# First-block loads gathered on the sync queue, and the stores of h moved, in a GELU layer with its gradients

## The chip, the cores and the metric

The kernel runs on one core of a Trainium2 chip. The metric is the device time of one execution in microseconds; lower is better. The engines are TensorE (PE in the profile, its weight loads PEld), VectorE (DVE), ScalarE (ACT), GpSimd (POOL) and SyncE (SP). DMAs are issued from SP, ACT or POOL; each of the three has a queue of its own, and all are carried out by the core's 16 DMA engines.

## The reference

A dense layer with GELU between two matrices, forward and backward, in bfloat16:

```python
B, S, D, F = 1, 2048, 448, 1792

def _fwd_reference(x, w1, b1, w2, b2):
    h = jnp.einsum("bsd,df->bsf", x, w1) + b1
    h = _gelu(h)                                   # tanh form
    return jnp.einsum("bsf,fd->bsd", h, w2) + b2

def reference(x, w1, b1, w2, b2, grad_out):
    _out, _vjp = jax.vjp(_f, x, w1, b1, w2, b2)    # _f is _fwd_reference
    return (_out, *_vjp(grad_out))                 # out, gx, gw1, gb1, gw2, gb2
```

## The kernel before

The 2048 rows are cut into four blocks of 512 (NB), and F into seven pairs of 128-row tiles (NPAIR), so there are 28 steps (NSTEP), step g being pair c of block b. The instructions of each engine stand in the order in which the code writes them (the schedule is manual), so every engine and every queue works through its own list in that order and waits where an operand is missing.

In step g, `M1(g + 1)` makes u = x w1 of the next step on TensorE (L200, 8 matmuls), ACT and DVE form h (kept transposed in hT, a ring of 12 pairs) and the pieces of GELU's derivative, `M4(g)` makes q = grad_out w2^T (L209, 8 matmuls), `dve_gate` multiplies q by the derivative into ghT, a ring of 14 pairs, and `run_pieces` (L262) adds 8 to 16 products to the output rows ("o" units: h times w2) and to the rows of x's gradient ("g" units: gh times w1T). In the first block only "o" units run, two products each per step, so that step g reads the w2 tiles 2g and 2g+1. "g" units, which read w1T, begin in step 7, the first of the second block.

M1 reads the transposed x block and w1; M4 reads the transposed grad_out block and w2T, a transposed copy of w2. `load_xg` brings a block of x or grad_out by two transposing DMAs on SP (L131, L132), `load_w2T` the columns f0:f1 of w2T by two on SP (L142, L143), `load_w1T` tiles of w1T by one on SP (L149). `load_w1` brings columns of w1 by two plain DMAs on a queue that it is given (L135, L136), and `load_w2` tiles of w2 by one (L139). In the kernel before, w1's first 256 columns and b1 come by ACT's queue, all other pieces of w1 and w2 by POOL's. POOL also sets the lower rows of w2T's last slice to zero after each piece of w2T has landed (`zero_w2T`, L146) and a row of ones under each block of x (`ones_row`, L152).

`store_h` writes one pair of h to DRAM from POOL (L238, 256 KB), and it stands three steps behind its step: `if g >= LAG: store_h(g - LAG)` with LAG = 3, the last three after the loop. POOL also stores the finished rows of both outputs (L281), two units at a time. `turn_gh` (L243) transposes gh on SP, SBUF to SBUF.

After the loop POOL loads all of x and grad_out (L352, L353), SP transposes h back from DRAM (L365), TensorE finishes the last block's units and makes the two weight gradients (L401, L409 and L420), DVE sums the bias gradients.

Of the kernel before, what the change touches and what calls it, by code (L numbers as in the profile page):

```python
# [18 lines left out]
def kernel(  # L19
# [15 lines left out]
    nc = tc.nc  # L35
    P = 128
    B, S, D = x.shape
    F = w1.shape[1]
    assert B == 1
    NS = S // P  # L40
    NF = F // P
# [7 lines left out]
    NPAIR = NF // 2  # L49
    assert DL == 64 and F % 256 == 0 and S % SB == 0 and NPAIR == 7 and NB == 4  # L50
    NSTEP = NB * NPAIR
# [44 lines left out]
    def xq(b):  # L96
        o = (b % 2) * 2 * KD * SB
        return xg_flat[:, o:o + KD * SB].rearrange("p (k s) -> p k s", k=KD)

    def gq(b):  # L100
        o = ((b % 2) * 2 + 1) * KD * SB
        return xg_flat[:, o:o + KD * SB].rearrange("p (k s) -> p k s", k=KD)
# [5 lines left out]
    def hT(g):  # L108
        return ring(hT_flat, HR, g)
# [19 lines left out]
    def load_xg(src, dst, b):  # L129
        rows = slice(b * SB, (b + 1) * SB)  # L130
        nc.sync.dma_start_transpose(out=dst[:, KF, :], in_=src[rows, DOV:D])  # L131
        nc.sync.dma_start_transpose(out=dst[:, 0:KF, :], in_=src[rows, 0:KF * P])  # L132

    def load_w1(eng, f0, f1):
        eng.dma_start(out=w1_sb[:, 0:KF, f0:f1], in_=w1[0:KF * P, f0:f1].rearrange("(k p) f -> p k f", p=P))  # L135
        eng.dma_start(out=w1_sb[DL:P, KF, f0:f1], in_=w1[KF * P:D, f0:f1])  # L136

    def load_w2(eng, t0, t1):
        eng.dma_start(out=w2_sb[:, t0:t1, :], in_=w2[t0 * P:t1 * P, :].rearrange("(t p) d -> p t d", p=P))  # L139

    def load_w2T(f0, f1):
        nc.sync.dma_start_transpose(out=w2T_sb[:, 0:KF, f0:f1], in_=w2[f0:f1, 0:KF * P])  # L142
        nc.sync.dma_start_transpose(out=w2T_sb[:, KF, f0:f1], in_=w2[f0:f1, DOV:D])  # L143

    def zero_w2T(f0, f1):
        nc.gpsimd.memset(w2T_sb[0:DL, KF, f0:f1], 0.0)  # L146

    def load_w1T(t0, t1):
        nc.sync.dma_start_transpose(out=w1T_sb[:, t0:t1, :], in_=w1[:, t0 * P:t1 * P])  # L149

    def ones_row(b):
        nc.gpsimd.memset(xq(b)[0:1, KF, :], 1.0)  # L152
# [4 lines left out]
    load_xg(x2, xq(0), 0)  # L157
    load_w1(nc.scalar, 0, 256)
    nc.scalar.dma_start(out=w1_sb[0:1, KF, :], in_=b1.rearrange("(o f) -> o f", o=1))
    load_w1(nc.gpsimd, 256, 512)  # L160
    ones_row(0)
    load_w2T(0, 256)
    load_xg(g2, gq(0), 0)
    load_w2(nc.gpsimd, 0, 2)
    load_w1(nc.gpsimd, 512, 768)
    pw = psum_a.tile([P, SB], F32, name="acc")
    for i in range(16):
        nc.tensor.matmul(pw[:], lhsT=warm[:, 0:P], rhs=warm, start=True, stop=True)
    zero_w2T(0, 256)
    load_w2(nc.gpsimd, 2, 6)  # L170
    load_w1(nc.gpsimd, 768, 1280)
    load_w2T(256, 768)
    zero_w2T(256, 768)
    load_w1(nc.gpsimd, 1280, F)
    load_w2(nc.gpsimd, 6, NF)
    load_w2T(768, F)
    zero_w2T(768, F)
    nc.gpsimd.dma_start(out=b2_bc[:], in_=b2.rearrange("(o d) -> o d", o=1).to_broadcast((P, D)))
    load_w1T(0, 4)
    load_xg(x2, xq(1), 1)  # L180
    ones_row(1)
    load_xg(g2, gq(1), 1)
    load_w1T(4, 8)
    load_w1T(8, 12)
# [3 lines left out]
    def blk(g):  # L188
        return divmod(g, NPAIR)
# [4 lines left out]
    def M1(g):  # L194
        b, c = blk(g)
        for h in range(2):
            fc = slice((2 * c + h) * P, (2 * c + h + 1) * P)
            u = psum_u.tile([P, SB], F32, name="u")
            for kt in range(KD):
                nc.tensor.matmul(u[:], lhsT=w1_sb[:, kt, fc], rhs=xq(b)[:, kt, :], start=(kt == 0), stop=(kt == KD - 1))  # L200
            u_of[g, h] = u

    def M4(g):
        b, c = blk(g)
        for h in range(2):
            fc = slice((2 * c + h) * P, (2 * c + h + 1) * P)
            q = psum_g.tile([P, SB], F32, name="q")
            for kt in range(KD):
                nc.tensor.matmul(q[:], lhsT=w2T_sb[:, kt, fc], rhs=gq(b)[:, kt, :], start=(kt == 0), stop=(kt == KD - 1))  # L209
            g_of[g, h] = q  # L210

    def act_first(g):
        for h in range(2):
            nc.scalar.activation(out=hT(g)[:, h, :], in_=u_of[g, h][:], func=ACT.Gelu_apprx_tanh)  # L214
            nc.scalar.activation(out=A_of(g)[:, h, :], in_=u_of[g, h][:], func=ACT.Square, scale=math.sqrt(3.0 * GELU_C * GELU_A))  # L215

    def dve_first(g):
        for h in range(2):
            nc.vector.scalar_tensor_tensor(out=B_of(g)[:, h, :], in0=A_of(g)[:, h, :], scalar=3.0 * GELU_C,  # L219
                                           in1=u_of.pop((g, h))[:], op0=ALU.add, op1=ALU.mult)  # L220
        nc.vector.scalar_tensor_tensor(out=p_of(g), in0=A_of(g), scalar=GELU_C, in1=hT(g), op0=ALU.add, op1=ALU.mult)  # L221

    def act_second(g):
        nc.scalar.activation(out=t_of(g), in_=B_of(g), func=ACT.Tanh, scale=-1.0 / 3.0)  # L224
        nc.scalar.activation(out=p_of(g), in_=p_of(g), func=ACT.Copy, bias=-0.5)  # L225

    def dve_second(g):
        nc.vector.tensor_scalar(out=t_of(g), in0=t_of(g), scalar1=1.0, scalar2=None, op0=ALU.add)
        nc.vector.tensor_tensor(out=t_of(g), in0=t_of(g), in1=p_of(g), op=ALU.mult)  # L229

    def dve_gate(g):
        for h in range(2):
            nc.vector.scalar_tensor_tensor(out=ghT(g)[:, h, :], in0=t_of(g)[:, h, :], scalar=1.0,  # L233
                                           in1=g_of.pop((g, h))[:], op0=ALU.add, op1=ALU.mult)

    def store_h(g):
        b, c = blk(g)
        nc.gpsimd.dma_start(out=hT_dram_v[:, 2 * c:2 * c + 2, b * SB:(b + 1) * SB], in_=hT(g))  # L238

    def turn_gh(b, c0, c1):  # L240
        o = ((b * NPAIR + c0) % GR) * 2 * SB
        n = 2 * (c1 - c0)
        nc.sync.dma_start_transpose(out=gh_nat[:, b, 2 * c0:2 * c1, :].rearrange("p t (j f) -> p (t j) f", f=P),  # L243
                                    in_=ghT_flat[:, o:o + n * SB])
# [40 lines left out]
    def run_pieces(units):  # L285
        for un in units:
            if un.piece():
                full.append(un)

    def flush():  # L290
        while full:
            evict(full.pop(0))
# [13 lines left out]
    for b in range(NB):  # L306
        for i, (c0, c1) in enumerate(GROUPS):
# [1 line left out]
            if b == NB - 1:  # L309
                at = b * NPAIR + (4, 5, 6)[i]  # L310
            turns.setdefault(at, []).append((b, c0, c1))
    LAG = 3

    M1(0)
    act_first(0)
# [3 lines left out]
    for g in range(NSTEP):  # L319
        b, c = blk(g)  # L320
        pieces = [U[k] for k in seq[b] for _ in range(NF)]
        n = len(pieces)
        own = pieces[n * c // NPAIR:n * (c + 1) // NPAIR]
        grown = [U[k] for k in grow[b] for _ in range(2)]
        cut = len(own) // 2
        if g + 1 < NSTEP:
            M1(g + 1)
            act_first(g + 1)
            dve_first(g + 1)
        if g >= LAG:  # L330
            store_h(g - LAG)
        flush()
        run_pieces(own[:cut] + grown[:len(grown) // 2])
        M4(g)
        dve_gate(g)
        flush()
        run_pieces(own[cut:] + grown[len(grown) // 2:])
        if g + 1 < NSTEP:
            act_second(g + 1)
            dve_second(g + 1)  # L340
        if c == 1 and 0 < b < NB - 1:
            load_xg(x2, xq(b + 1), b + 1)
            ones_row(b + 1)
            load_xg(g2, gq(b + 1), b + 1)
        for t in turns.get(g, []):
            turn_gh(*t)
    for g in range(NSTEP - LAG, NSTEP):
        store_h(g)
    flush()

# [111 lines left out]
```

## Time and profile before

| | us |
|---|---|
| median of 3 runs | 304.62 |
| the three runs | 304.72, 304.62, 297.37 |
| the profiled execution | 295.46 |
| its span, first to last instruction | 293.5 |
| PE busy | 275.9 (94%) |
| DVE busy | 184.2 (63%) |
| ACT busy | 139.9 (48%) |
| POOL busy | 62.3 (21%) |
| mean granted TensorE clock | 0.980 |

The page of the profile gives busy times, then the span in 40 slices of 7.34 us with a digit for the busy tenths of each engine, the granted TensorE clock and the DMA engines; then the DMA queues, the chain of work that ended last, and the costliest groups of instructions. SP's transposes (queue q1) moved 23.93 MB and took 46.8% of the 16 DMA engines' span, POOL's queue (q0) 17.78 MB and 20.1%, ACT's (q10) 1.84 MB and 2.1%. "SPq" and "ACTq" are the issuing instructions of those queues; "w_gw" is the tile that holds w2 (later its gradient), "w_x" the one of w1 (later x), "w2T_g" that of w2T (later grad_out), "w1T_gw" that of w1T, "xg_h" that of the transposed blocks.

### The profile page before, as it was taken

Reading aid. Unit: us, or ns where it says so; the run is one execution under the profiler, and the core shown is the slowest. Engines: PE = TensorE matmul, PEld = TensorE weight load, DVE = VectorE, ACT = ScalarE, POOL = GpSimd, SP = SyncE. Lnnn points to the kernel's source line nnn. Section 1 sums busy time; section 2 is a strip of 40 time slices with the busy share of each in tenths; the row PEclk is TensorE's granted clock in tenths of the full one; section 3 lists DMA queues with packets and bytes.
Section 4 is the critical chain, followed back from the end, with each engine's and each line's share of the span. In section 5 each row is a group of like instructions: output and inputs, shape, how many; then the busy total and the mean of one; then the engine's idle time right before and its main releaser. Section 6 shows DMA issues by size and latency. Waiting matters only on the chain.

```text
span 293.5 us, 3609 instructions
## 1 busy us (share of the span) xinstructions
PE 275.9 (94%) x1392; PEld 134.0 (46%) x1392; DVE 184.2 (63%) x245; ACT 139.9 (48%) x213; POOL 62.3 (21%) x73
## 2 busy tenths in 40 slices
PE   7898089989999999999999999999999999999995
PEld 2343034444444444444444444555444565555552
DVE  1599328998888899888877876111999995000000
ACT  1778407777877777778766673002102211111211
POOL 5331040024040040302201204500060004900000
PEclk9999759999999999999999999999999999999999
DMA  8999999699653299732715245999999971011111
GB/s 152 233 241 165 124 209 224 79 162 267 100 176 71 58 244 174 207 58 103 175 37 138 50 128 174 193 294 348 238 213 220 274 156 47 7 50 47 47 43 38
DMA packets 98547, 43.78 MB, mean 149 GB/s; under 512 B 90081, under 2 KB 94401, under 8 KB 98530
## 3 DMA queue, kind: packets, MB, share of 16 engines
q1 hardware_dynamic: 90720, 23.93, 46.8%
q0 software_dynamic: 5408, 17.78, 20.1%
q10 hardware_dynamic: 2402, 1.84, 2.1%
q8 instruction: 11, 0.18, 0.3%
q14 instruction: 6, 0.05, 0.1%
HBM read 7.00 MB, written 14.23 MB: 72 GB/s over the span
## 4 chain that ended last, share of the span: by engine, by line
PE 79%; DMA 8%; SPq 4%; DVE 3%; ACT 3%; issue 1%; POOL 1%; DVEq 0%
PE acc L262 25%; PE acc L420 14%; PE q L209 13%; PE acc L401 12%; PE u L200 11%; DMA w_gw<-in_w_dram 6%; DMA w2T_g<-in_w_dram 2%; PE acc L409 2%; DVE T L221 2%; SPq L142 1%; SPq L132 1%; ACT hT_h L214 1%; ACT A L215 1%; SPq L131 1%; ACT T L225 1%
## 5 line engine op out<-in xcount | busy, mean ns | idle before, releaser
L262 PE MATMUL acc<-w_gw,hT_h 128*128 128x448 bf16 x224 | 49.8, 356 | 10.5 <-DMA w_gw<-in_w_dram 9.8
L209 PE MATMUL q<-xg_h,w2T_g 128*128 128x512 bf16 x224 | 54.8, 388 | 0.7 <-POOL w2T_g L146 0.4
L219 DVE SCALAR_TENSOR_TENSOR Bt<-A,u 128x512 f32<-128x512 f32 x56 | 38.4, 687 | 26.1 <-ACT A L215 25.3
L200 PE MATMUL u<-xg_h,w_x 128*128 128x512 bf16 x224 | 53.0, 379 | 1.7 <-DVE Bt L219 1.0
L214 ACT ACTIVATE hT_h<-u 128x512 bf16<-128x512 f32 x56 | 33.6, 599 | 33.9 <-PE u L200 33.9
L262 PE MATMUL acc<-w1T_gw,ghT_h 128*128 128x448 bf16 x224 | 47.4, 353 | 0.0
L233 DVE SCALAR_TENSOR_TENSOR ghT_h<-T,q 128x512 bf16<-128x512 bf16 x56 | 36.0, 682 | 12.3 <-PE q L209 12.3
L224 ACT ACTIVATE T<-Bt 128x1024 bf16<-128x1024 f32 x28 | 29.6, 1057 | 17.5 <-DVE Bt L219 17.5
L262 PEld LDWEIGHTS <-hT_h 128*128 128x128 bf16 x224 | 22.1, 99 | 33.3 <-issue 12.1
L401 PE MATMUL acc<-gh_nat,w_x 128*128 128x512 bf16 (+1 forms) x192 | 36.7, 353 | 0.0
L209 PEld LDWEIGHTS <-w2T_g 128*128 128x128 bf16 x224 | 22.2, 100 | 27.2 <-issue 2.3
L200 PEld LDWEIGHTS <-w_x 128*128 128x128 bf16 x224 | 21.9, 98 | 27.2 <-issue 2.5
L221 DVE SCALAR_TENSOR_TENSOR T<-A,hT_h 128x1024 bf16<-128x1024 f32 x28 | 34.1, 1218 | 0.0
L215 ACT ACTIVATE A<-u 128x512 f32<-128x512 f32 x56 | 33.8, 604 | 0.0
L262 PEld LDWEIGHTS <-ghT_h 128*128 128x128 bf16 x224 | 21.9, 98 | 22.1 <-issue 0.2
L225 ACT ACTIVATE T<-T 128x1024 bf16<-128x1024 bf16 x28 | 29.6, 1057 | 2.2
L386 DVE TENSOR_TENSOR A<-A,gh_nat 128x1792 f32<-128x1792 f32 x14 | 30.0, 2142 | 0.5
L430 DVE CAST w_gw<-acc 128x224 bf16<-128x224 f32 x1 | 0.4, 393 | 43.9 <-ACT w_gw L429 43.9
L401 PEld LDWEIGHTS <-w_x 128*128 128x128 bf16 x192 | 18.7, 98 | 17.8 <-issue 0.4
L422 ACT CAST w_gw<-acc 128x448 bf16<-128x448 f32 x13 | 6.9, 532 | 32.6 <-PE acc L420 32.6
L229 DVE TENSOR_TENSOR T<-T 128x1024 bf16<-128x1024 bf16 x28 | 19.4, 692 | 3.3 <-ACT T L225 0.5
L281 POOL DMA_DIRECT2D out_dram<-io_g x8 | 5.8, 726 | 72.1 <-ACT io_g L277 72.1
(40 smaller groups left out, 191.4 us busy)
## 6 DMA issues: line engine op xcount, KB each, us to landing
hT_dram<-hT_h POOLq DMA_DIRECT2D x28, 256.0 KB, 3.2
out_dram<-io_o POOLq DMA_DIRECT2D x8, 224.0 KB, 5.1
out_dram<-io_g POOLq DMA_DIRECT2D x8, 224.0 KB, 3.5
w_x<-in_x_dram POOLq DMA_DIRECT2D x1, 1792.0 KB, 12.8
w2T_g<-in_grad_out_dram POOLq DMA_DIRECT2D x1, 1792.0 KB, 16.6
out_dram<-w_gw SPq DMA_DIRECT2D x4, 336.0 KB, 2.4
w_gw<-in_w_dram POOLq DMA_DIRECT2D x1, 896.0 KB, 17.3
w_x<-in_w_dram POOLq DMA_DIRECT2D x2, 384.0 KB, 6.1
```

The costliest lines, as they stand in the source:

```text
L200: nc.tensor.matmul(u[:], lhsT=w1_sb[:, kt, fc], rhs=xq(b)[:, kt, :], start=(kt == 0), stop=(kt == KD - 1))
L209: nc.tensor.matmul(q[:], lhsT=w2T_sb[:, kt, fc], rhs=gq(b)[:, kt, :], start=(kt == 0), stop=(kt == KD - 1))
L214: nc.scalar.activation(out=hT(g)[:, h, :], in_=u_of[g, h][:], func=ACT.Gelu_apprx_tanh)
L215: nc.scalar.activation(out=A_of(g)[:, h, :], in_=u_of[g, h][:], func=ACT.Square, scale=math.sqrt(3.0 * GELU_C * GELU_A))
L219: nc.vector.scalar_tensor_tensor(out=B_of(g)[:, h, :], in0=A_of(g)[:, h, :], scalar=3.0 * GELU_C, in1=u_of.pop((g, h))[:], op0=ALU.add, op ...
L221: nc.vector.scalar_tensor_tensor(out=p_of(g), in0=A_of(g), scalar=GELU_C, in1=hT(g), op0=ALU.add, op1=ALU.mult)
L225: nc.scalar.activation(out=p_of(g), in_=p_of(g), func=ACT.Copy, bias=-0.5)
L233: nc.vector.scalar_tensor_tensor(out=ghT(g)[:, h, :], in0=t_of(g)[:, h, :], scalar=1.0, in1=g_of.pop((g, h))[:], op0=ALU.add, op1=ALU.mult)
L262: nc.tensor.matmul(self.ps[:, 0:D], lhsT=lhsT, rhs=rhs, start=(ft == 0), stop=(ft == NF - 1))
L386: nc.vector.tensor_tensor(out=gsb_v, in0=gsb_v, in1=gh_rows(st, 0, NF), op=ALU.add)
L401: nc.tensor.matmul(psv, lhsT=x_all[:, st, kt * P:(kt + 1) * P], rhs=gh_rows(st, a0, a1), start=(st == 0), stop=(st == NS - 1))
L420: nc.tensor.matmul(ps[:, 0:D], lhsT=h_blk[ft][:, st, :], rhs=g_all[:, st, :], start=(st == 0), stop=(st == NS - 1))
```

## The change

All loads of w1 and w2 that POOL issued go to SP, and they are put among SP's transposes: each piece stands beside the piece of w2T of about the same step. x of the second block now comes ahead of the first piece of w1T. The stores of h no longer trail by three steps: none is issued before step 6, the last of the first block, then up to two per step until they have caught up (0 and 1 in step 6, 2 and 3 in step 7, and so on to 8 and 9 in step 10), then one per step, one step behind. One store is left after the loop.

```diff
     load_xg(x2, xq(0), 0)
     load_w1(nc.scalar, 0, 256)
     nc.scalar.dma_start(out=w1_sb[0:1, KF, :], in_=b1.rearrange("(o f) -> o f", o=1))
-    load_w1(nc.gpsimd, 256, 512)
+    load_w1(nc.sync, 256, 512)
     ones_row(0)
     load_w2T(0, 256)
+    load_w2(nc.sync, 0, 2)
     load_xg(g2, gq(0), 0)
-    load_w2(nc.gpsimd, 0, 2)
-    load_w1(nc.gpsimd, 512, 768)
+    load_w1(nc.sync, 512, 768)
...
     zero_w2T(0, 256)
-    load_w2(nc.gpsimd, 2, 6)
-    load_w1(nc.gpsimd, 768, 1280)
     load_w2T(256, 768)
+    load_w2(nc.sync, 2, 6)
+    load_w1(nc.sync, 768, 1280)
     zero_w2T(256, 768)
-    load_w1(nc.gpsimd, 1280, F)
-    load_w2(nc.gpsimd, 6, NF)
     load_w2T(768, F)
+    load_w1(nc.sync, 1280, F)
+    load_w2(nc.sync, 6, NF)
     zero_w2T(768, F)
     nc.gpsimd.dma_start(out=b2_bc[:], in_=b2.rearrange("(o d) -> o d", o=1).to_broadcast((P, D)))
-    load_w1T(0, 4)
     load_xg(x2, xq(1), 1)
     ones_row(1)
+    load_w1T(0, 4)
     load_xg(g2, gq(1), 1)
...
-    LAG = 3
+    stored = 0
...
-        if g >= LAG:
-            store_h(g - LAG)
+        for _ in range(2):
+            if g >= NPAIR - 1 and stored < g:
+                store_h(stored)
+                stored += 1
...
-    for g in range(NSTEP - LAG, NSTEP):
+    for g in range(stored, NSTEP):
         store_h(g)
```

## The prediction

> **What bounds the kernel now.** I read the page first, then the chain of waits, then the waits by total, then windows cut at the gap. The page says that TensorE is busy 94% of the span, and its slices say where the other 6% is:
>
> ```profile
> PE 275.9 (94%) x1392; PEld 134.0 (46%) x1392; DVE 184.2 (63%) x245; ACT 139.9 (48%) x213; POOL 62.3 (21%) x73
> PE   7898089989999999999999999999999999999995
> PEclk9999759999999999999999999999999999999999
> DMA  8999999699653299732715245999999971011111
> ```
>
> A slice is 7.34 us. PE has one empty slice, the fifth (29 to 37 us), and in it and the next the granted clock falls to 0.7 and 0.5. From about 65 us on PE is full to the end (224.96 of 225.03 us between 64.97 and 290.00). So a change of the loads can only give what PE loses before 65 us. The chain names the owner of the gap:
>
> ```profile
> 20.84 17.27 DMA w_gw<-in_w_dram
> 38.11 0.04 issue
> 38.15 1.65 PE acc L262 x4
> 39.80 3.35 PE q L209 x8
> 43.15 0.76 PE acc L262 x4
> ```
>
> The load of w2's tiles 6 to 13 (L139, issued by POOL at 20.84) takes 17.27 us, and the products of step 3, which read tiles 6 and 7, wait for it. The list of waits has it as one wait, and the windows show the DMA engines full but slow in it:
>
> ```profile
> PE acc L262 <- DMA w_gw<-in_w_dram: 9.8, 1, 9.8
> 2.00:26.00 24.00, 21.64 (x93) 9.32 (x92) 14.46 (x23) 15.53 (x23) 8.27 (x14) 1.00 1.10 224
> 28.20:38.15 9.95, 0.16 (x1) 0.00 (x0) 3.64 (x6) 4.14 (x7) 0.00 (x0) 0.73 1.19 110
> 38.15:43.00 4.85, 4.85 (x13) 1.74 (x13) 0.69 (x1) 0.00 (x0) 3.23 (x5) 0.50 1.29 221
> ```
>
> The last three columns are the granted clock, the DMA share and GB/s: 224 GB/s before the gap, 110 in it, when POOL's w2 load shares the engines with SP's transposes of w1 and of the second x block, which nobody needs before 43 us.
>
> **What the gap is worth.** PE would have begun those products at 26.47 + 1.73 = 28.20 us (the matmuls of step 4's u, eight at the chain's pitch). It began at 38.15, 9.95 us late, and then ran at half clock: four products took 1.65 us instead of 0.76, eight of q 3.35 instead of 1.73, another 2.51. PE therefore works as if it had resumed at 28.20 + 9.95 + 2.51 = 40.66 us at full clock. The gain is 40.66 less the new time of resuming.
>
> **The issue order.** Seven loads (w1 in four pieces of two DMAs each, w2 in three of one: eleven DMAs) leave POOL for SP. Ahead of w2 6:14 on SP stand, new, ten plain DMAs: w1 256:512, 512:768, 768:1280 and 1280:F (two each), w2 0:2 and 2:6. The same kind on ACT's queue, and SP's own times now:
>
> ```profile
> 0.74 0.46 ACTq L135 DMA_DIRECT2D w_x<-in_w_dram  x1
> 1.24 0.53 ACTq L136 DMA_DIRECT2D w_x<-in_w_dram  x1
> ...
> 8.82 1.55 SPq L132 DMA_TRANSPOSE xg_h<-in_grad_out_dram  x1
> 10.42 2.02 SPq L142 DMA_TRANSPOSE w2T_g<-in_w_dram  x1
> 12.48 1.26 SPq L143 DMA_TRANSPOSE w2T_g<-in_w_dram  x1
> 13.79 5.50 SPq L142 DMA_TRANSPOSE w2T_g<-in_w_dram  x1
> 19.34 1.30 SPq L143 DMA_TRANSPOSE w2T_g<-in_w_dram  x1
> 20.68 3.11 SPq L149 DMA_TRANSPOSE w1T_gw<-in_w_dram  x1
> ```
>
> At 0.5 us each the ten cost SP 5.0 us. SP now finishes w2T at 20.64, so the big w2 load is issued at about 25.6, later than POOL's 20.84, but with nothing unneeded beside it. Each DMA on the hardware queues also waits for the one eight places earlier; by the landings below none of these waits ends later than SP gets there.
>
> **When w2 6:14 lands.** No row shows a plain load in SP's line behind transposes, so I bound it. Early bound, by bytes: x and grad_out of the first block 0.52 MB each (512 columns, 64 read twice), w2T 1.84, w1 1.61, w2 1.61, in all 6.10 MB; at 224 GB/s from 2.0 us that ends at 29.2. Late bound, by issue: 25.6, plus 6.7 us to landing (the w2T piece issued at 19.34 took that), plus 2.1 for the 0.46 MB by which this load exceeds the next smaller one at 224 GB/s: 34.4. The middle is 31.8, and I take it: both rows are equally near.
>
> **What the ten issues delay earlier.** grad_out's first block is issued at 8.82 + 3 x 0.5 = 10.3; with its 4.6 us to landing M4 of step 0 starts at 14.9, not 13.44: 1.5 us late. The w2T piece of step 1 goes out at 12.48 + 2.5 = 15.0, lands after its 6.5 us at 21.5, POOL's memset of 0.52 us follows, and M4 of step 1 goes on at 22.1 instead of 19.66: 2.4 late. These delays do not add to the end while PE waits for w2 6:14 anyway: PE arrives at step 3's products at 29.7 to 30.6 and waits 1 to 2 us. That wait is the cover; without it 1.5 to 2.4 us are paid, which sets the earliest resume at 29.7. At the late bound PE waits 4.7 us; the trace has PE stop at 28.36 and a mean clock of 0.68 between 32 and 34 us, so it fell some 4.3 us after the stop, and there up to 2.5 us come back.
>
> **What follows.** x of block 1, grad_out of block 1 and w1T now follow w2 (x ahead of the first w1T piece). They are 2.66 MB, plus 0.52 for two stores: at 224 GB/s from 31.8 they are done at 46, at 110 GB/s at 61. Needed, by today's PE times less 8.9 us: x at about 45, the first w1T piece at 51.5 (60.44 today), w1T's third at 58 (67.07). At the higher rate all are in time; at 110 GB/s the third piece lands at 58.5, a loss near 0.5 us, which I set to 0.
>
> **POOL and the stores.** POOL loses eleven issues of 0.54 to 0.94 us, about 8 us, at nothing: POOL was no bound, only its memsets feed PE, and they wait for transposes. The 28 stores of h (0.72 us of POOL, 0.26 MB each) all remain. Today POOL issues four from 40.28; after the change two, before POOL stops for the first output rows. That spares w1T 0.52 MB, 2.3 us of DMA, inside the cover above. In blocks 1 to 3 a store trails by one step instead of three; its slot of h is reused twelve steps later, so ACT gets no wait. At the end one store follows the loop instead of three; x and grad_out for the weight gradients wait for PE, not for POOL (1.06 us idle on a PE release at 186.20). Gain 0.
>
> **A rule against it.** The Trainium skill, "DMA: Bandwidth & Descriptors", section "Rules for kernel authors", says that spreading DMAs over SP, ACT and GpSimd brings no bandwidth since all run on the same 16 engines, but saves the sequencers' issue time. Read so, collecting them on one queue can only lose issue time; then the late bound holds and the sum is 295.46 - 6.3 = 289.2. The trace shows the other side, the order: with two queues at work the load that PE needed took 17.27 us, where w2 2:6, half its size, had taken 4.9.
>
> **The sum.** Resume 31.8 against 40.66: 8.9 us. The profiled execution took 295.46 us (span 293.5, 1.96 around it): 286.6. The runs shown stand at 304.62 in the middle, the lowest at 297.37, 1.9 above the profiled one. Only the loads' stretch has idle PE time that can vary, so I expect the excess of the two long runs to sit there and to go; I carry the 1.9: **288.5 us**.
>
> **Rivals.**
> - *The stall stays, in another place.* The 110 GB/s may belong to the DMA side after 26 us whatever the queue. One line also lets the long w2T piece (5.50 us of issue) hold back all behind it. If w2 6:14 lands at 36.5 and the clock falls, PE resumes in effect at 39.0: gain 1.7, 293.8 on the profiled basis, 295.7 with the 1.9. For it: a DMA share over 1.0 throughout. Against: the same engines gave 221 GB/s right after, with POOL's stores and SP's transposes together. 0.15.
> - *Slower: the second block's operands come too late.* They stand behind everything in one line. It loses from the point where w1T's third piece lands after 67.1; 2.94 MB up to it from 31.8 makes that 83 GB/s. At 70 GB/s it lands at 73.8: 6.7 us and 2.5 of half clock, 304.7, with the 1.9 306.6. For it: 86 GB/s stood between 28 and 33 us. Against: 221 right after the gap. 0.09.
> - The forecast: 0.76.
>
> **Range and chances.** The earliest resume, 29.7, gives 295.46 - 11.0 = 284.5; I go to 283.5 because the early delays are estimates. The late bound with the clock lost gives 295.46 - 3.8 + 1.9 = 293.6; the likeliest case alone spans 284 to 294. To take in the first rival, and long runs that keep part of their excess, the range goes to 298. About 2% is what a measurement of this kernel can tell from no change; 0.76 of faster, 0.14 within, 0.10 slower: nearly all of the forecast is more than 2% faster, the first rival is within, the second slower.
>
> **What would show it.** Right: the wait of L262 for the w2 load under 3 us, the load issued by SP near 25 and landed near 32, the slices of PE without a 0, no 0.5 in the clock row, u of step 5 on PE near 35 instead of 43.74, and the shift of 9 us unchanged to the end. Wrong: a wait of PE for w1T or x near 45 to 58, w2 6:14 landing after 36, or PE's products after 65 us no longer back to back.

## The result and the profile after

The changed kernel took 286.66 us (median of 4 runs, 285.96 to 287.19); the kernel before, with one more run, 302.69 (297.37 to 304.72). The two medians are 16 us apart. The ratio, 0.9584 with a 95% interval of 0.9484 to 0.9683, tells a smaller gain, about 4%, because it counts only those runs of the kernel before that lie near its fastest (297.37 and 300.75). The prediction was 288.5 with a range of 283.5 to 298.0. The profiled execution took 286.44 us with a span of 284.7, so between the two profiled executions the span shrank by 8.8 us; the sum had said 8.9. What the medians differ by beyond that is the excess of the longer runs of the kernel before, to which e2 below returns.

The slices of the page after, in the order PE, granted clock, DMA engines:

```profile
PE   8789699899999999999999999999999999999995
...
PEclk9999999999999999999999999999999999999999
DMA  7899997899632998434531724999999971011111
```

The empty slice of PE is gone, the fifth now has a 6, and the row of the clock shows no fall. The chain of waits after, around the load that had made the gap (start, us, what):

```profile
17.15 4.42 SPq L142
...
24.12 7.64 DMA w_gw<-in_w_dram
31.76 0.04 issue
31.81 0.92 PE acc L262 x4
32.73 1.73 PE q L209 x8
```

The load of w2 6:14 now goes out at 24.12 instead of 20.84, later than before, and takes 7.64 us instead of 17.27. PE begins step 3's products at 31.81, at full clock at once: four take 0.92 us and eight of q 1.73, where they had taken 1.65 and 3.35. The line of the waits by total (us, times, longest):

```profile
PE acc L262 <- DMA w_gw<-in_w_dram: 3.9, 2, 2.6
```

Two windows (the last three columns are clock, DMA share, GB/s):

```profile
2.00:26.00 24.00, 21.20 (x88) 9.14 (x88) 14.19 (x22) 15.64 (x23) 2.01 (x4) 1.00 0.99 209
...
28.20:38.15 9.95, 7.37 (x35) 3.41 (x35) 6.92 (x11) 6.44 (x11) 1.96 (x3) 1.00 1.24 217
```

The stretch that had moved 110 GB/s moves 217. The first one moves a little less than before, 209 against 224. PE's wait for w2 is 3.9 us in two pieces instead of 9.8 in one. PE's timeline names both (start, us, engine, line, what, and in brackets the idle time before and its releaser):

```profile
13.48 1.89 PE L209 MATMUL q<-xg_h,w2T_g 128*128 128x512 bf16 x8 [0.42 <-DMA xg_h<-in_grad_out_dram]
...
19.16 0.92 PE L262 MATMUL acc<-w_gw,hT_h 128*128 128x448 bf16 x4 [1.30 <-DMA w_gw<-in_w_dram]
...
27.36 1.89 PE L200 MATMUL u<-xg_h,w_x 128*128 128x512 bf16 x7
31.81 0.92 PE L262 MATMUL acc<-w_gw,hT_h 128*128 128x448 bf16 x4 [2.56 <-DMA w_gw<-in_w_dram]
```

SP's own times, to be set against the ones shown of before:

```profile
9.57 1.52 SPq L132 DMA_TRANSPOSE xg_h<-in_grad_out_dram  x1
...
12.30 1.79 SPq L142 DMA_TRANSPOSE w2T_g<-in_w_dram  x1
14.13 1.26 SPq L143 DMA_TRANSPOSE w2T_g<-in_w_dram  x1
15.44 0.58 SPq L139 DMA_DIRECT2D w_gw<-in_w_dram  x1
...
17.15 4.42 SPq L142 DMA_TRANSPOSE w2T_g<-in_w_dram  x1
21.61 1.30 SPq L143 DMA_TRANSPOSE w2T_g<-in_w_dram  x1
```

### The profile page after: what moved, and what is told of

The parts are those of the page before. It is cut to its first block, busy times and chain, and to the rows that moved or that the text cites. A ratio compares the mean times of both kernels' runs of the same rounds, so it can differ in the third digit from the quotient of the medians.

```text
span 284.7 us, 3596 instructions
## 1 busy us (share of the span) xinstructions
PE 273.1 (96%) x1377; PEld 133.8 (47%) x1392; DVE 184.1 (65%) x245; ACT 140.0 (49%) x213; POOL 54.2 (19%) x62
## 4 chain that ended last, share of the span: by engine, by line
PE 80%; SPq 8%; DVE 3%; ACT 3%; DMA 3%; issue 1%; DVEq 0%
PE acc L262 26%; PE acc L422 15%; PE acc L403 13%; PE q L209 13%; PE u L200 12%; DMA w_gw<-in_w_dram 3%; SPq L142 3%; PE acc L411 2%; DVE T L221 2%; SPq L143 1%; SPq L132 1%; ACT hT_h L214 1%; ACT A L215 1%; SPq L131 1%; SPq L135 1%
## 5 line engine op out<-in xcount | busy, mean ns | idle before, releaser
L200 PE MATMUL u<-xg_h,w_x 128*128 128x512 bf16 x212 | 52.2, 379 | 1.6 <-DVE Bt L219 1.0
L262 PE MATMUL acc<-w_gw,hT_h 128*128 128x448 bf16 x224 | 49.1, 352 | 4.6 <-DMA w_gw<-in_w_dram 3.9
L209 PE MATMUL q<-xg_h,w2T_g 128*128 128x512 bf16 x221 | 52.6, 379 | 0.5 <-DMA xg_h<-in_grad_out_dram 0.4
L238 POOL DMA_DIRECT2D hT_dram<-hT_h x28 | 20.0, 716 | 7.8 <-ACT hT_h L214 7.7
```

What stands on the lines that cost most here:

```text
L262: nc.tensor.matmul(self.ps[:, 0:D], lhsT=lhsT, rhs=rhs, start=(ft == 0), stop=(ft == NF - 1))
```

## The experiments

Every time below is a median, with the lowest and the highest run of that kernel in brackets. Ratios are to runs of the kernel before on the same chip, with their 95% intervals. The chips differ from one group of experiments to the next, so a difference of a few tenths of a microsecond between medians of two experiments says nothing.

**Loads alone (e1) and stores alone (e2).** Which half of the change carries the gain? e1 is the changed kernel with the old stores:

```diff
-    stored = 0
+    LAG = 3
...
-        for _ in range(2):
-            if g >= NPAIR - 1 and stored < g:
-                store_h(stored)
-                stored += 1
+        if g >= LAG:
+            store_h(g - LAG)
```

> The loads as after the change, the stores of h as before it (three steps behind). Theory, the loads carry the whole gain: PE resumes step 3's products near 31.8 us as after the change, and the time is 286.7 us, within 0.5 of the changed kernel; its runs lie close together (within 1.5 us), since the loads' stretch is where the long runs of the kernel before have their excess. Rival, the stores carry part of it (fewer stores in front of w1T's transposes): a new wait of PE for w1T near 51 to 58 us and 288 to 290 us.

Measured: 286.04 us (285.67 to 286.26), ratio 0.9599 (0.9567 to 0.9631); PE waits 1.13 and 2.11 us for w2 and resumes at 31.63. That x of the second block now stands ahead of the first piece of w1T was not tried by itself; it is part of e1. e2 is the reverse: the loads of before, the stores of after.

> The stores as after the change, the loads as before it. Theory: PE still waits 9 to 11 us for the w2 load of tiles 6 to 13 near 28 us, its clock falls to 0.5, and the time is that of the kernel before, 295 to 305 us with the same spread of some 7 us between runs. Rival, the stores matter: over 2 us faster than the kernel before in the same rounds, with the w2 wait unchanged, so that the difference lies after 43 us.

Measured: 297.56 us (293.33 to 307.19), ratio 0.9893 (0.9827 to 0.9959). So the loads carry the gain. Beside the new loads the stores change nothing that can be told (ratio 0.9584 with them, 0.9599 without); beside the old loads the spread of 14 us is too wide to read a per cent from it.

e2's profile is of its longest run, 307.19 us, and shows where the excess of that run sits. Its wait for w2:

```profile
PE acc L262 <- DMA w_gw<-in_w_dram: 19.9, 2, 12.6
```

and two pieces of its chain:

```profile
12.72 14.54 DMA w2T_g<-in_w_dram
...
29.07 21.45 DMA w_gw<-in_w_dram
```

The same loads that took 6.55 and 17.27 us in the profile of before took 14.54 and 21.45 here. PE resumed at 50.56 us instead of 38.15, 12.4 us later, and the span of 305.4 us is 11.9 longer. From 60 us on PE was busy for 239.25 of 240.00 us at a clock of 1.00. So in this run the whole excess lies in the loads' stretch. The runs without a profile fit this, but show no more than their clock: 32 runs of the kernel before on three chips lay between 291.36 and 306.97, with mean granted clocks from 0.988 down to 0.964, the longest with the lowest; those of the changed kernel and e1 spread 1.2 and 0.6 us, with clocks of 0.998 to 1.0.

**POOL's queue, but earlier (e3).** The old load was issued at 20.84, because POOL's memset waited for a transpose ahead of it. Is the late issue the cause?

```diff
     load_w1(nc.gpsimd, 768, 1280)
+    load_w1(nc.gpsimd, 1280, F)
+    load_w2(nc.gpsimd, 6, NF)
     load_w2T(256, 768)
     zero_w2T(256, 768)
-    load_w1(nc.gpsimd, 1280, F)
-    load_w2(nc.gpsimd, 6, NF)
```

> The kernel before with POOL's last three loads (w1 1280:F and w2 6:14) put ahead of the memset that waits for w2T 256:768, so that POOL issues the w2 load near 14 us instead of 20.84; the queue stays POOL's. Theory 1, the load was late because it was still under way when transposes that nobody needs yet joined it: it lands before 24 us, PE's wait at 28 us is gone or under 2 us, and the time is 283 to 288 us, without the sync queue. Theory 2, loads of POOL's queue beside transposes are slow in themselves: the load takes over 12 us again and lands after 26, with a time of 288 to 295 us. Theory 3, the moved loads only push the w2T transposes back: PE's wait goes to q of step 3 (w2T 768:1792) and the time lies between, 287 to 291 us.

Measured: 292.62 us (290.37 to 297.34), ratio 0.9799 (0.9733 to 0.9865). The load went out at 15.69 and took 15.4 us. PE's timeline:

```profile
31.13 0.92 PE L262 MATMUL acc<-w_gw,hT_h 128*128 128x448 bf16 x4 [1.59 <-DMA w_gw<-in_w_dram]
34.00 0.82 PE L209 MATMUL q<-xg_h,w2T_g 128*128 128x512 bf16 x3 [1.95 <-DMA w2T_g<-in_w_dram]
36.14 2.31 PE L209 MATMUL q<-xg_h,w2T_g 128*128 128x512 bf16 x5 [1.32 <-POOL w2T_g L146]
```

Theory 1 falls, and what theories 2 and 3 say of the waits holds together (the time, 292.62, lies in theory 2's range and above theory 3's): issued five microseconds earlier, the load still took 15.4 us, while the transpose of w2T beside it was pushed back (POOL's memset behind it ran at 35.13, in the profile of before at 26.05).

**The transposes held back (e4).** Is it the company that makes POOL's load slow? One tiny DMA ahead of SP's unneeded transposes waits for the load:

```diff
+    nc.sync.dma_start(out=gate_d[0:1, 0:64], in_=w2_sb[0:1, NF - 1, 0:64])
     load_w1T(0, 4)
     load_xg(x2, xq(1), 1)
```

> The kernel before, with one small DMA put on SP ahead of the first w1T piece that reads a row of w2's last tile, so that SP's transposes of w1 and of the second x block wait until POOL's load of w2 6:14 has landed; every queue stays as it was. Theory A, two queues at work slow each other: with nothing beside it but the rest of w2T the load lands 7 to 10 us after its issue near 20.8 (at 28 to 31 us), PE's wait falls from 9.8 to under 3 us, and the time is 285 to 288 us. Theory B, POOL's loads are slow in themselves at that place: over 14 us to landing again and no gain, 295 us or more, plus what the held transposes then cost.

Measured: 287.52 us (285.56 to 290.95), ratio 0.9642 (0.9568 to 0.9716). The page's line of the load (the last number is the time from issue to landing) and PE's longest wait:

```profile
w_gw<-in_w_dram POOLq DMA_DIRECT2D x1, 896.0 KB, 8.7
22.61 2.00 PE L211 MATMUL q<-xg_h,w2T_g 128*128 128x512 bf16 x5 [2.64 <-POOL w2T_g L147]
```

The load landed 8.7 us after its issue, and PE did not wait for it. The issue itself came only at 23.80, since the piece of w2T ahead of it took 9.58 us and not 6.55, so that the load landed at 32.5, later than expected; PE, held up by the memset behind that piece, reached step 3's products at 32.84. Of the two theories A fits: without the unneeded transposes beside it the load took half its time, and most of the gain comes back with the loads still on POOL's queue. That any two queues would slow each other does not follow; e6 and e6c ask that.

**One queue, other order (e5).** On SP, but w2 6:14 behind the second x block and the first w1T piece:

```diff
-    load_w2(nc.sync, 6, NF)
...
     load_w1T(0, 4)
+    load_w2(nc.sync, 6, NF)
     load_xg(g2, gq(1), 1)
```

> The changed kernel with the load of w2 6:14 moved on SP behind the second x block and the first w1T piece, so that all is on one queue but not in order of need. Theory, order in the line is a cost of its own: the load is issued near 33 us and lands near 37, PE waits about 8 us for it and its clock falls, so that it resumes in effect near 39.5, and the time is 286.7 + 7.7 = 294 us. Rival, one queue is what counts and order little: the load lands before 34 and the time stays under 289.

Measured: 294.69 us (293.92 to 295.86), ratio 0.99 (0.9867 to 0.9933), too near 1 to call it faster. Its chain:

```profile
31.37 5.90 DMA w_gw<-in_w_dram
37.27 0.04 issue
37.31 1.65 PE acc L262 x4
38.96 2.96 PE q L209 x8
```

The load itself is quick (5.90 us), but it starts 7.25 us later than in the changed kernel; PE waits 7.46 us, the clock falls (1.65 us for four products), and the median is 8.0 us above the changed kernel's (the profiled spans, 292.2 and 284.7, differ by 7.5). Being on one queue is not enough: with this one load out of order nearly the whole gain is lost.

**A second hardware queue (e6, e6c).** Only w2 6:14 moves, from POOL to ACT.

> The kernel before with the load of w2 6:14 alone moved from POOL's queue to ACT's, issued by ACT behind step 1's second half at about 18.4 us; SP's transposes keep their order and start as before. Theory C, it is POOL's queue that suffers beside transposes: from ACT's queue the load lands within 8 us, PE's wait for it is under 2 us, and the time is 284 to 288 us. Theory A, any second queue beside the transposes suffers: it takes over 10 us, lands after 28.5, PE waits again and the time is 289 to 296 us.

Measured: 295.2 us (292.59 to 300.09), no interval. As a version to keep it missed: ACT issued the load only at 28.05 us, and ACT's own work stood behind it.

```profile
28.05 0.39 ACTq L139 DMA_DIRECT2D w_gw<-in_w_dram  x1
28.49 0.60 ACT L206 ACTIVATE hT_h<-u 128x512 bf16<-128x512 f32 x1 [10.12 <-DMA w2T_g<-in_w_dram]
```

What ACT waited for was the landing of one of SP's w2T transposes, whose data the load does not need: a DMA signals its landing by a semaphore, a counter that others wait on, and the load had been given the same one as that transpose. PE then waited 6.35 us for DVE, which needs ACT. The load itself took 7.5 us beside SP's transposes of the second x block and of grad_out. Put behind step 0's second half, it had no long wait:

```diff
-    load_w2(nc.gpsimd, 6, NF)
...
     act_second(0)
     dve_second(0)
+    load_w2(nc.scalar, 6, NF)
```

> The kernel before with the load of w2 6:14 alone on ACT's queue, issued by ACT right behind step 0's second half, near 13.5 us, where it has to wait only for a DMA that has landed by then (in the run before with ACT's queue the load stood behind one that landed at 28 us). It is issued about as early as in the run with POOL's loads put forward (15.69 us, 15.4 us to landing, w2T 768:F landed at 35), so that the two differ in the queue. Theory C, POOL's queue beside transposes is the slow pair: from ACT the load lands within 9 us (by 23), w2T 768:F by 29, and the time is 284 to 288 us. Theory A, any second queue beside transposes is slow: over 12 us to landing, w2T 768:F after 32, 289 to 293 us.

Measured: 287.75 us (284.99 to 289.55), ratio 0.9575 (0.9457 to 0.9693). From ACT at 13.66 the load took 9.9 us, a little over the 9 expected, and the memset behind the last w2T piece ran at 29.38, not at 35.13 as in e3. Windows over the loads' time, in e3 and then in e6c:

```profile
16.00:31.00 15.00, 12.80 (x61) 5.79 (x60) 14.13 (x22) 12.28 (x19) 1.12 (x2) 1.00 1.16 177
```

```profile
14.00:24.00 10.00, 8.07 (x39) 3.53 (x37) 8.81 (x13) 8.24 (x12) 1.77 (x3) 1.00 1.13 266
```

Each window covers about the time that the load was under way. Over e3's own window, 16 to 31 us, e6c moved 256 GB/s against 177. No wait for w2 is left on PE; its longest is 1.93 us for the memset behind w2T 256:768. Theory C is the nearer one, and e6's 7.5 us agree: from ACT the load did not suffer beside transposes as it did from POOL. There is a reserve: e3 also had w1 1280:F moved forward, so the two are not exact twins.

This changes the reading of the whole change. One load moved to another queue, and all else left as it was, gave a ratio (0.9575) that the four runs cannot tell from the changed kernel's 0.9584. Gathering the loads on one queue is a way to the gain, not the only one.

**Two better versions (v1, v2).** The two waits left in the changed kernel are for pieces of w2 behind longer pieces of w2T. v1 cuts the pieces by step:

```diff
-    load_w2T(256, 768)
-    load_w2(nc.sync, 2, 6)
-    load_w1(nc.sync, 768, 1280)
-    zero_w2T(256, 768)
-    load_w2T(768, F)
-    load_w1(nc.sync, 1280, F)
-    load_w2(nc.sync, 6, NF)
-    zero_w2T(768, F)
+    load_w2(nc.sync, 2, 4)
+    load_w2T(256, 768)
+    load_w1(nc.sync, 768, 1280)
+    load_w2(nc.sync, 4, 8)
+    zero_w2T(256, 768)
+    load_w2T(768, 1280)
+    load_w2(nc.sync, 8, NF)
+    load_w1(nc.sync, 1280, F)
+    zero_w2T(768, 1280)
+    load_w2T(1280, F)
+    zero_w2T(1280, F)
```

> The changed kernel with its loads cut so that each step's share comes first: w2 2:4 ahead of w2T 256:768, w2 4:8 ahead of the next w2T piece, w2T 768:F in two pieces with w2 8:14 and w1 1280:F between. Theory, the two waits left in the changed kernel (1.30 us for w2 2:6 in step 1 and 2.56 us for w2 6:14 in step 3) are a matter of order alone: both go under 0.5 us and the time is 283 us, 3.4 to 3.9 less than the changed kernel. Rival, the line is full and the wait only moves to w2T (q of step 1 or 3) or to grad_out: 285.5 to 287 us.

Measured: 283.08 us (282.94 to 285.18), ratio 0.952 (0.9479 to 0.9562): 3.6 us less than the changed kernel (3.0 less than e1, which ran on the same chip), near the two waits (1.30 + 2.56). No wait for w2 is left in its profile; that profile is of the longest of its runs, 285.18, and its largest wait is

```profile
PE q L212 <- DMA xg_h<-in_grad_out_dram: 2.1, 1, 2.1
```

Short as this wait is, the clock fell behind it (0.50 between 16.5 and 18.5 us, four products in 1.70 us), while after the changed kernel's wait of 2.56 us it did not.

v2 takes w1 256:512 off SP (`load_w1(nc.scalar, 0, 512)`) to bring grad_out earlier.

> The version by need (v1) with w1 256:512 loaded by ACT together with 0:256, so that SP issues two DMAs less ahead of grad_out's first block. Theory: grad_out's block is issued about 1.3 us earlier and PE's wait for it (2.1 us in v1's profile, 0.42 in the changed kernel's) goes to zero: 282 to 282.7 us, 0.4 to 1 less than v1. Rival, ACT's larger load slows x's transposes at the start and u of step 0 begins later than 7.4 us: no gain, 283 to 284 us.

Measured: 283.7 us (283.43 to 283.91), ratio 0.9535 (0.9484 to 0.9587): no gain over v1. PE's wait for grad_out is 0.27 us, u of step 0 begins at 7.50 as before, so the rival named the number and not the reason; a wait of 1.32 us for DVE's eviction came up at 48.73 instead.

## Why the prediction held, step by step

**The gap and what it is worth.** Right. PE worked as if it had resumed at 40.66 us; it now resumes at 31.81. The difference of 8.85 is the change of the span, 8.8.

**The landing of w2 6:14.** Right in the number, and that it was right to 0.01 us is luck: 31.8 was the middle of two bounds 5.2 us apart, and each was off by about 2.6 us. In the late bound both terms were too long. The ten plain DMAs took 5.45 us of issue (0.49 to 0.58 each) where I had 5.0, but SP reached the load at 24.12, not 25.6, because the three w2T transposes that stand ahead were issued faster (1.28, 1.79 and 4.42 us instead of 2.32, 2.02 and 5.50). The load then took 7.64 us, less than the 8.8 of the late bound. That 8.8 was itself put together wrongly: the 6.7 us in it belong to a piece of w2T of 0.26 MB, and counted from that piece the load has 0.66 MB more, not 0.46, which would have made the bound 35.2 and the middle 32.2. The early bound counted only the bytes that were needed first, at 224 GB/s; the engines moved 209 up to 26 us, and the second block's x transposes, issued at 24.75 and 26.80, ran beside the load.

**The early delays.** Here two terms were wrong. grad_out's first block was to come 1.5 us late and came 0.04 late (13.48 against 13.44): it was issued 0.75 us later, not 1.5, and landed sooner. The 2.4 us for w2T's second piece were not paid there either; what came late was w2 2:6, moved from POOL's 11.36 to SP's 15.44, a wait of 1.30 us in step 1 that the working did not list. PE therefore arrived at step 3 at 27.36 + 1.73 = 29.09, not 29.7 to 30.6, and waited 2.56 instead of 1 to 2. As foreseen, the later wait swallowed it; v1, where both are gone, shows what the two are worth together. The prediction let a wait cost half clock only from some 4.3 us on, as the trace of before had it; in v1 and in e4 the clock fell behind waits of 2.10 and 2.64 us, so that the 1 to 2 us of wait which it called free were free here, but need not have been.

**What follows.** Right. The second x block's transpose issued at 26.80 landed 7.6 us later, at 34.4, with u of step 7 beginning at 44.98; the last w1T piece, issued at 41.27, had landed by 46.3 (none of the four took over 5.0). u of step 5 began at 35.04 (35 forecast). PE has no wait for w1T or x.

**POOL and the stores at nothing.** Right as far as can be told: e1 is the changed kernel without the stores' part, at 286.04 against 286.66.

**The 1.9 us carried for runs without a profile.** Wrong size. The sum without it, 286.6, is the measured median; the changed kernel's runs lie from 0.5 below to 0.8 above the profiled one. The reason given, that the excess of long runs sits in the loads' stretch and would go, fits e2's long run and the small spread after the change, and it left nothing to carry.

**The rule that spoke against the change.** The Trainium skill ("DMA: Bandwidth & Descriptors", "Rules for kernel authors") has it that spreading DMAs over the issuing engines brings no bandwidth and saves only issue time. In the first 24 us that agrees with the trace: with POOL's loads beside SP's transposes the engines moved 224 GB/s, with these loads on SP 209. In the stretch of the gap it does not: 110 GB/s with POOL's load beside SP's transposes, 217 with the load on SP. So the queue that issues a load can matter much, and the measurements decide for this case.

**The mechanism.** The prediction put the slow load down to two queues at work and to the order in the line. That order and unneeded company cost time, e5 and e4 show. That any second queue is slow, e6 and e6c speak against: from ACT the same load took 7.5 and 9.9 us beside transposes, from POOL 17.27 and, issued early, 15.4. What sets POOL's loads apart stays open.

**The rivals.** That the stall would stay because the DMA side is slow after 26 us is refuted by the same stretch at 217 GB/s. That the second block's operands would come late did not happen: x was there ten microseconds early, and all of w1T before PE's first product with it at 51.75.

## To carry to other kernels

When a wait for a load ends the chain, look at what else the DMA engines carry in that time and when that is needed: here transposes that nobody read before 43 us stood beside a load that PE needed at 28. Three cures gave about the same median: all on SP's queue in order of need (286.66), the unneeded transposes held back (e4, 287.52), and the one load issued early from ACT (e6c, 287.75). Two half measures did not: POOL's load issued earlier, but still beside transposes (e3, 2%), and one queue out of order (e5, 1%). Of the three cures the one queue had the closest runs, 1.2 us apart against 5.4 and 4.6, on four runs each. Then cut the pieces so that each step's share comes first, which here was worth another 3.6 us.

## What the hardware showed that I had not expected

- While the load of w2 6:14 was under way, POOL's queue and SP's transposes together moved less than the other arrangements: 134 GB/s over the 17.27 us of the load before, and 177 in e3, against 223 with all on SP and 266 with the load on ACT. It is not so at all times (224 GB/s between 2 and 26 us in the kernel before). Why was not settled; it was not tried whether it is POOL's descriptors, the transposes, or where they write.
- SP's issue of a transpose is not a fixed cost: the 1024-column piece of w2T took 5.50 us in the profile of before, 12.22 in e3 and 13.56 in e2, with POOL's loads about, 9.38 in e6c with a load on ACT as well, and 4.42 in the changed kernel.
- A DMA on ACT can be held by an unrelated transpose of SP that has the same semaphore (issue at 28.05 in e6, where 18.4 was expected), and then ACT's arithmetic waits with it.
- The clock can fall behind a wait of 2.10 us (v1) and stay up behind one of 2.56 us (the changed kernel). What decides between them no run here shows.
